# Summing an expert layer back into PSUM and keeping a PSUM bank as scratch for the ordering

## The chip, the cores and the metric

The kernel runs on one core of a Trainium2 chip. The metric is the device time of one execution in microseconds (us). The core's engines work side by side, each through its own list of instructions in order: TensorE (PE in the rows) does matmuls into PSUM, VectorE (DVE) and ScalarE (ACT) read and write SBUF and PSUM, GpSimd (POOL) works on SBUF, SyncE (SP) issues DMAs. An instruction waits for semaphores that others raise.

## The reference

Three parts follow one another: attention with a threshold (2 batches, 8 heads, 576 positions, head size 64), a mixture of experts over the 1152 tokens that come out, and a dense layer with a maximum over three products. The middle one is where the change lies:

```python
def _moe_ref(x, w_gate, w1, w2, capacity):      # x: 1152 x 512, 8 experts, hidden size 1024
    logits = x @ w_gate
    expert_idx = np.argmax(logits, axis=1)
    # softmax; gate_w[i] = probability of the chosen expert
    for i in range(N):                          # tokens take the places of their expert in order
        e = expert_idx[i]
        if counts[e] < capacity:
            disp[e, counts[e]] = x[i]; pos[i] = counts[e]; counts[e] += 1; keep[i] = True
    h = np.maximum(np.einsum('ecd,edf->ecf', disp, w1), 0.0)
    y = np.einsum('ecf,efd->ecd', h, w2)
    # out[i] = gate_w[i] * y[expert_idx[i], pos[i]] for the tokens that are kept
```

## The kernel before

**Stages.** Attention runs to about 190 us. Then comes the routing (gate, places of the tokens), then the ordering: the experts are sorted by a key made of their numbers of tokens, the sorted numbers go into `table`, and lists say which tokens each expert gets. The experts run as eight ranks, `rank(r)` with r from 0 to 7, in the order of the sort; rank r computes `WIN[r]` columns (128, 256, 192, 176, 160, 144, 128, 224 tokens). A branch on a flag, for experts with more tokens than their window, stands ahead of rank 7 (L1333, L1334). The dense stage runs from about 395 us to the end.

**Precision.** Every fp32 operand is split into a rounded high part and a rest, the low part. A product is three matmuls: high weights by high and low data, low weights by high data. Where the columns c are below 256, high and low data lie side by side and one matmul (L1178) fills 2c columns of a PSUM bank, another (L1182) adds the third product to the first c. The two halves of the bank have to be added afterwards. With 256 columns (rank 1) three matmuls (L1180 to L1182) go into the same c columns and nothing is left to add.

**A rank.** Layer 1 has eight pieces f of 128 hidden units (`piece1`), each with a PSUM bank of its own from the pool `ps_h` (six banks, tile `ho`), and four steps k of a matmul pair. `evac1` empties it: ScalarE copies the upper half to `t2` (L1191), VectorE adds the lower half into an SBUF tile `hs` (L1193), and then, two pieces later (the list `later`), ScalarE writes the relu as the high part of `hl` (L1198) and VectorE the low part as max(hs, 0) less the high part (L1199). Layer 2 has four pieces d of eight steps; step k of layer 2 needs piece k of `hl`.

**Weights.** Four 1 MB DMAs a rank (issued by SyncE, tile `raw_w`, three buffers) bring them. Each gives two units: ScalarE rounds the high part (`hi_part`, L872), then VectorE or GpSimd in turn subtracts for the low part (`lo_part`, L877), both into `ring_u`. The DMA of rank r's weights is issued with an expert number read from `table`. After the low part of a unit's second half the next DMA is issued.

**The ordering.** `order1` sorts the experts by counting compares on 8 x 8 matrices (`gtm`, `mr`) up to the CAST into `table` (L739); `spread(1)` has five small matmuls (L629) that build the token map; `order2`, `order2b`, `gates(1)` and `order3` are generators whose steps are laid between the pieces of ranks 0 to 3, one a piece. `order3` ends with ten compare rows (L828) that feed ten small matmuls (L824). The routing has one PSUM bank of its own (`ps_r`, tile `tp`). The order of all instructions is fixed by the order of the code.

Of the kernel before, what the change touches and what calls it, by code (L numbers as in the profile page):

```python
# [76 lines left out]
def fused_kernel(ctx, tc, qk, v, tau, wg, w1, w2, cap, m1, m2, m3, mo, out):  # L77
# [518 lines left out]
    def spread(b):  # L596
# [35 lines left out]
        if b == 0:  # L632
            dve.tensor_copy(tmp0, tm)
            owner.pop()
        else:
# [121 lines left out]
    def order2():  # L757
        f0, f1 = carve([(E, NJ, E), (E, NJ)])
        dve.tensor_tensor(out=f0, in0=tmap.unsqueeze(1).to_broadcast([P, E, NJ, E]),
# [5 lines left out]
        dve.tensor_tensor(out=go, in0=gtm, in1=cnt.unsqueeze(1).to_broadcast([P, E, E]), op=ALU.mult)  # L765
        dve.tensor_reduce(out=off.unsqueeze(2), in_=go, axis=AX.X, op=ALU.add)
        yield
        pick(1, off, rp)
        dve.tensor_copy(table[:, 0, E:2 * E], srt[:, 1])
        yield  # L770

    def order2b():
        pick(2, cnt, rp)
        yield

# [3 lines left out]
        om = smt("om", [P, E])  # L779
# [1 line left out]
        dve.tensor_tensor(out=ov[:, 1], in0=wide(2), in1=st_f, op=ALU.subtract)
        dve.tensor_tensor(out=ov[:, 0], in0=wide(1), in1=st_f, op=ALU.add)
# [2 lines left out]
        dve.tensor_scalar(out=ov[:, 1], in0=ov[:, 1], scalar1=0.0, scalar2=None, op0=ALU.max)
        dve.tensor_scalar(out=ov[:, 0], in0=ov[:, 0], scalar1=float(NT), scalar2=None, op0=ALU.min)
        yield
        om1 = smt("om1", [P, 1])
        dve.tensor_reduce(out=om1, in_=om, axis=AX.X, op=ALU.max)
        dve.tensor_copy(ovt, ov)  # L790
        dve.tensor_copy(flag_t, om1)
# [3 lines left out]
    def order3():  # L795
        n = B * 5
        t2, sl, ge, sg, ind, sp_, gl = carve([(n, E), (n,), (n, NJ + 1), (n,), (n, NJ), (n,), (n, 2)])
# [536 lines left out]
    with tc.If(flag > 0):  # L1334
        iw_i = tq.tile([P, OW], I32, name="mk", bufs=1)
        pool.iota(iw_i, pattern=[[1, OW]], base=0, channel_multiplier=0)
        iw = tq.tile([P, OW], F32, name="hs", bufs=4)
# [11 lines left out]
        def over_chunk(r, m):  # L1349
# [121 lines left out]
```

## Time and profile before

| | |
|---|---|
| median of 3 timed runs | 544.28 us (543.66 to 544.32) |
| profiled execution | 547.7 us, of which the span of the trace is 545.9 |
| busy: TensorE, VectorE, ScalarE, GpSimd | 87%, 67%, 50%, 50% of the span |
| TensorE busy 200 to 226, 250 to 275, 330 to 364 us | 19.33 of 26, 22.01 of 25, 27.45 of 34 us |
| TensorE busy 395 us to the end | 145.34 of 151 us |

How to read the rows. A timeline row has the start in us from the beginning of the span, the duration in us, engine, line, operation, output and inputs by the program's names, shape and count, and in brackets the idle time of the engine just before it with what ended it. A row of waits says which engine's instruction on which tile and line waited for which other one. A row of windows has the stretch and its length, busy time with the number of instructions, the granted clock of TensorE as a share of full speed, the share of the DMA engines' time and GB/s. A group of instructions has the line, the shapes and the count, then busy us and the mean duration in ns, then idle time before. The names: `hl` is the split output of layer 1, `ho` a PSUM bank, `hs` the sum in SBUF, `ring_u` split weights, `table` the sorted expert numbers.

### The profile page before, as it was taken

What the parts mean: (1) busy time and instruction counts of PE and PEld (TensorE: products, weight loads), DVE (VectorE), ACT (ScalarE), POOL (GpSimd) and SP (SyncE); (2) the same over time, 40 slices, a digit from 0 to 9 for tenths busy, and PEclk for the clock granted to TensorE, in tenths of its full rate; (3) what the DMA queues carried; (4) which work ended last, traced back from release to release, by engine and by line L of the source; (5) the groups of instructions that cost most, each with busy time, mean ns of one, the idle gap of its engine ahead of it and who ended that gap; (6) DMA issues with size and microseconds to landing.
All of it is one profiled execution on the core that took longest, in us unless ns stands there. A gap on an engine that the chain in (4) does not pass through costs nothing. (4 is left out here: it accounts for less than half of the span.)

```text
span 545.9 us, 10050 instructions
## 1 busy us (share of the span) xinstructions
PE 477.6 (87%) x3752; PEld 411.9 (75%) x3752; DVE 366.6 (67%) x800; ACT 274.4 (50%) x522; POOL 274.6 (50%) x265
## 2 busy tenths in 40 slices
PE   6688885997785986999799999877999999999995
PEld 4355553674464856999799898777899999999884
DVE  5989989888964249898887867729854454359100
ACT  3879998875644133744466686634412112125211
POOL 3768878886550118572456765646513112217422
PEclk9969999898877577799799999889999999999999
DMA  8577937597598305493737867852024222320111
GB/s 290 120 199 167 202 88 205 127 205 161 114 240 182 112 9 193 155 300 127 246 106 230 272 209 238 278 164 78 1 78 140 91 77 85 148 77 1 58 59 58
DMA packets 105707, 80.42 MB, mean 147 GB/s; under 512 B 66528, under 2 KB 93280, under 8 KB 105392
## 3 DMA queue, kind: packets, MB, share of 16 engines
q1 hardware_dynamic: 100256, 65.97, 42.3%
q10 hardware_dynamic: 3728, 8.47, 5.4%
q0 software_dynamic: 1664, 5.24, 2.7%
q8 instruction: 31, 0.51, 0.4%
q14 instruction: 28, 0.23, 0.1%
HBM read 58.74 MB, written 4.72 MB: 116 GB/s over the span
## 5 line engine op out<-in xcount | busy, mean ns | idle before, releaser
L877 POOL TENSOR_TENSOR ring_u<-raw_w,ring_u 128x1024 fp32r<-128x1024 f32 x32 | 84.5, 2641 | 104.7 <-ACT ring_u L872 102.5
L343 POOL TENSOR_TENSOR phl<-p_t,phl 128x512 f16<-128x512 f32 (+1 forms) x138 | 98.5, 740 | 40.1 <-ACT phl L335 39.8
L1178 PE MATMUL ho<-hl,ring_u 128*128 128x256 f32 (+5 forms) x224 | 69.9, 382 | 12.7 <-DVE hl L1199 11.2
L255 PE MATMUL ps<-kq 64*128 64x288 f32 (+1 forms) x320 | 63.8, 527 | 16.4 <-DVE p_t L280 8.6
L872 ACT ACTIVATE ring_u<-raw_w 128x1024 fp32r<-128x1024 f32 x64 | 66.1, 1054 | 9.2 <-DMA raw_w<-in_moe_w_dram 9.2
L275 ACT ACTIVATE e_t<-ps,negm 128x576 f32<-128x576 f32 x72 | 53.3, 740 | 27.2 <-DVE s_sb L264 24.5
L1140 POOL TENSOR_TENSOR ring_u<-bits_a,ring_u 128x1024 fp32r<-128x1024 f32 x12 | 29.2, 2432 | 74.6 <-ACT ring_u L1139 74.6
L1182 PE MATMUL ho<-hl,ring_u 128*128 128x128 f32 (+6 forms) x256 | 64.8, 253 | 0.0
L264 DVE TENSOR_SCALAR_CACHE_REDUCE s_sb<-ps 128x576 f32<-128x576 f32 x72 | 53.6, 745 | 12.3 <-PE ps L255 12.1
L280 DVE SCALAR_TENSOR_TENSOR p_t<-ps,thr,e_t 128x576 f32<-128x576 f32 x72 | 58.5, 812 | 1.2 <-POOL phl L343 0.6
L1178 PEld LDWEIGHTS ho<-hl,ring_u 128*128 128x128 f32 x224 | 45.7, 204 | 17.5 <-DVE hl L1199 15.0
L1178 PE MATMUL ho<-xl,ring_u 128*128 128x384 f32 (+5 forms) x192 | 55.9, 369 | 3.3 <-DVEq L1334 3.3
L1182 PE MATMUL ho<-xl,ring_u 128*128 128x256 f32 (+6 forms) x224 | 56.9, 254 | 0.0
L387 PEld LDWEIGHTS <-pT 128*128 128x128 f16 x1064 | 41.3, 103 | 16.1 <-issue 9.4
L1182 PEld LDWEIGHTS ho<-hl,ring_u 128*128 128x128 f32 x256 | 52.6, 205 | 0.0
L387 PE MATMUL av<-vah,pT 128*128 128x65 f16 (+1 forms) x684 | 45.2, 202 | 8.0 <-DMA pT<-phl 5.4
L335 ACT ACTIVATE phl<-p_t 128x576 f16<-128x576 f32 x69 | 47.3, 685 | 5.1 <-DVE p_t L280 4.9
L255 PEld LDWEIGHTS ps<-kq 64*128 64x128 f32 (+1 forms) x320 | 25.3, 205 | 27.1 <-DVE p_t L280 10.1
L1182 PEld LDWEIGHTS ho<-xl,ring_u 128*128 128x128 f32 x224 | 44.9, 200 | 0.0
L877 DVE TENSOR_TENSOR ring_u<-raw_w,ring_u 128x1024 fp32r<-128x1024 f32 x32 | 41.1, 1292 | 3.6 <-ACT ring_u L872 3.6
L1178 PEld LDWEIGHTS ho<-xl,ring_u 128*128 128x128 f32 x192 | 38.1, 198 | 4.0 <-ACTq L1334 3.5
L1199 DVE SCALAR_TENSOR_TENSOR hl<-hs,hl 128x128 fp32r<-128x128 f32 (+5 forms) x56 | 36.4, 650 | 5.6 <-ACT hl L1198 5.4
(277 smaller groups left out, 1121.6 us busy)
## 6 DMA issues: line engine op xcount, KB each, us to landing
raw_w<-in_moe_w_dram SPq DMA_DIRECT2D x29, 1024.0 KB, 5.5
raw_w<-in_moe_w_dram SPq DMA_DIRECT2D x18, 512.0 KB, 4.3
kq<-in_qk_dram ACTq DMA_DIRECT2D x3, 1728.0 KB, 7.8
raw_w<-in_moe_w_dram ACTq DMA_DIRECT2D x3, 1024.0 KB, 15.0
raw_w<-in_moe_w_out_dram SPq DMA_DIRECT2D x3, 1024.0 KB, 4.8
raw_w<-in_v_dram SPq DMA_DIRECT2D x2, 1024.0 KB, 10.3
kq<-in_qk_dram SPq DMA_DIRECT2D x2, 864.0 KB, 8.3
xd<-xn SPq DMA_DIRECT2D x1, 1024.0 KB, 5.8
```

What stands on the lines that cost most here:

```text
L255: pe.matmul(o, q[r, hh, t * P:min(t * P + P, S)], q[r, hh, S:S + SH], start=True, stop=True)
L264: dve.tensor_scalar(out=wide(s), in0=s_ps[i][:, :, 0:288], scalar1=-0.125, scalar2=None, op0=ALU.mult, op1=ALU.min, accum_out=m)
L275: act.activation(wide(e), s_ps[i][:, :, 0:288], AF.Exp, bias=negm[i], scale=0.125)
L280: dve.scalar_tensor_tensor(out=wide(p), in0=s_ps.pop(i)[:, :, 0:288], scalar=thr.pop(i), in1=wide(e_t.pop(i)), op0=ALU.is_ge, op1=ALU.mult)
L335: act.activation(phl[i][:, i % 2, 0:S], p_t[i], AF.Copy)
L343: pool.tensor_tensor(out=t[:, lo:hi], in0=p[:, src], in1=t[:, src], op=ALU.subtract)
L387: pe.matmul(o[0:m], pf[:, c * P + off:c * P + off + m], r, start=(n == 0), stop=(n == len(seq) - 1), skip_group_check=True)
L872: act.activation(u[:, 0], w, AF.Copy)
L877: lo_eng(i).tensor_tensor(out=u[:, 1], in0=w, in1=u[:, 0].bitcast(F32), op=ALU.subtract)
L1178: pe.matmul(o[:, 0:2 * c], whi(k), x(k), start=(k == 0), stop=False, skip_group_check=True)
L1182: pe.matmul(o[:, 0:c], wlo(k), x(k)[:, 0:c], start=False, stop=(k == last), skip_group_check=True)
L1199: dve.scalar_tensor_tensor(out=h[:, c:2 * c], in0=src, scalar=0.0, in1=h[:, 0:c].bitcast(F32), op0=ALU.max, op1=ALU.subtract)
```

## The change

The sum of layer 1 goes back into the PSUM bank (`o[:, 0:c]`), and relu and low part read it from there; the SBUF tile `hs` is gone. The bank is held until the low part is written. Seven banks rotate in place of six. The routing's bank `tp` is kept as scratch after the routing: count, token map, a copy of the constant row `iota_p`, the sorted values, offsets, overflow values, keys and gate sums are views of it (`bank`), so that the small operations of the ordering have one input in PSUM; operands change places where needed. ScalarE gets one copy (the constant row), VectorE two (`key` and `ov`, which are needed in SBUF as well).

```diff
     def gate_tail():
         assert not owner
         gate_open(1)
+        bank("ind", 0, 2 * 5, NJ)
+        bank("cnt", 10 * E, E)
+        w = bank("tmap", P, NJ, E)
+        for name, sh in (("iota", (P,)), ("srt", (3, E)), ("off", (E,)), ("om", (E,)), ("sl", (10,)), ("om1", (1,)),
+                         ("su", (5,)), ("key", (E,)), ("k1", (E,)), ("ov", (2, E, NCH))):
+            w = bank(name, w, *sh)
+        assert w <= 512
...
     def order1():
         k0 = smt("k0", [P, E])
-        dve.scalar_tensor_tensor(out=k0, in0=cnt, scalar=8.0, in1=iota_e, op0=ALU.mult, op1=ALU.subtract)
-        yield
-        k1 = smt("k1", [P, E])
+        dve.scalar_tensor_tensor(out=k0, in0=bk["cnt"], scalar=8.0, in1=iota_e, op0=ALU.mult, op1=ALU.subtract)
+        act.activation(bk["iota"], iota_p, AF.Copy)
+        yield
+        k1 = bk["k1"]
...
-        dve.tensor_tensor(out=key, in0=key, in1=k1, op=ALU.add)
-        yield
-        dve.tensor_tensor(out=gtm, in0=key.unsqueeze(1).to_broadcast([P, E, E]),
+        keyp, ie = bk["key"], bk["iota"][:, 0:E]
+        dve.tensor_tensor(out=keyp, in0=k1, in1=key, op=ALU.add)
+        dve.tensor_copy(key, keyp)
+        yield
+        dve.tensor_tensor(out=gtm, in0=keyp.unsqueeze(1).to_broadcast([P, E, E]),
                           in1=key.unsqueeze(2).to_broadcast([P, E, E]), op=ALU.is_gt)
...
-        dve.tensor_tensor(out=mr, in0=pos.unsqueeze(1).to_broadcast([P, E, E]),
-                          in1=iota_e.unsqueeze(2).to_broadcast([P, E, E]), op=ALU.is_equal)
+        dve.tensor_tensor(out=mr, in0=ie.unsqueeze(2).to_broadcast([P, E, E]),
+                          in1=pos.unsqueeze(1).to_broadcast([P, E, E]), op=ALU.is_equal)
...
-        dve.tensor_reduce(out=srt[:, 0].unsqueeze(2), in_=m_, axis=AX.X, op=ALU.add)
-        yield
-        dve.tensor_copy(table[:, 0, 0:E], srt[:, 0])
+        dve.tensor_reduce(out=bk["srt"][:, 0].unsqueeze(2), in_=m_, axis=AX.X, op=ALU.add)
+        yield
+        dve.tensor_copy(table[:, 0, 0:E], bk["srt"][:, 0])
...
-            dve.tensor_scalar(out=am2[:, t % 3], in0=iota_p, scalar1=sp_[:, t:t + 1], scalar2=None, op0=ALU.is_equal)
+            dve.tensor_scalar(out=am2[:, t % 3], in0=bk["iota"], scalar1=sp_[:, t:t + 1], scalar2=None, op0=ALU.is_equal)
...
-    ps_h = ctx.enter_context(tc.tile_pool(name="ps_h", bufs=6, space=PSUM))
+    ps_h = ctx.enter_context(tc.tile_pool(name="ps_h", bufs=7, space=PSUM))
...
             act.activation(t2[:, 0:c], o[:, c:2 * c], AF.Copy)
-            hs_ = tq.tile([P, 256], F32, name="hs", bufs=4)
-            dve.tensor_tensor(out=hs_[:, 0:c], in0=o[:, 0:c], in1=t2[:, 0:c], op=ALU.add)
-            src = hs_[:, 0:c]
-        else:
-            src = o[:, 0:c]
+            dve.tensor_tensor(out=o[:, 0:c], in0=o[:, 0:c], in1=t2[:, 0:c], op=ALU.add)
+        src = o[:, 0:c]
+
         def rest():
             act.activation(h[:, 0:c], src, AF.Relu)
```

The order of instructions changes in two places. The first is VectorE at the end of `order1` and the start of rank 0 (`ring_u` is the low part of a weights unit, `table` the sorted expert numbers, `tp` the routing's bank); before, from the compare `gtm` on:

```order
L725 TENSOR_TENSOR gtm<-key 128x64
L729 TENSOR_REDUCE pos<-gtm 128x8
L731 TENSOR_TENSOR mr<-pos,iota_e 128x64
L735 TENSOR_TENSOR m_3225<-mr,iota_e 128x64
L737 TENSOR_REDUCE srt<-m_3225 128x8
L739 CAST table<-srt 128x8
L877 TENSOR_TENSOR ring_u<-raw_w,ring_u 128x1024
L1193 TENSOR_TENSOR hs<-ho,t_3289 128x128
L877 TENSOR_TENSOR ring_u<-raw_w,ring_u 128x1024
L1193 TENSOR_TENSOR hs<-ho,t_3309 128x128
```

The same stretch of VectorE now:

```order
L748 TENSOR_TENSOR gtm<-tp,key 128x64
L752 TENSOR_REDUCE pos<-gtm 128x8
L754 TENSOR_TENSOR mr<-tp,pos 128x64
L758 TENSOR_TENSOR m_3223<-tp,mr 128x64
L1216 TENSOR_TENSOR ho<-ho,t_3287 128x128
L760 TENSOR_REDUCE tp<-m_3223 128x8
L901 TENSOR_TENSOR ring_u<-raw_w,ring_u 128x1024
L762 CAST table<-tp 128x8
L901 TENSOR_TENSOR ring_u<-raw_w,ring_u 128x1024
L1216 TENSOR_TENSOR ho<-ho,t_3306 128x128
```

The add of piece 0 and one subtraction of weights stand ahead of the CAST now; the subtraction is that of another unit than the one that followed the CAST before.

The second place is TensorE in rank 0, layer 1 (`x_` is the data, `tp<-bm,am` the five matmuls of the token map); before, in piece 0 behind its first pair:

```order
L629 LDWEIGHTS am
L629 MATMUL tp<-bm,am 128x80
L629 LDWEIGHTS am
L629 MATMUL tp<-bm,am 128x80
L1178 MATMUL ho<-x_95,ring_u 128x256
L629 LDWEIGHTS am
L629 MATMUL tp<-bm,am 128x80
L1182 MATMUL ho<-x_95,ring_u 128x128
```

Now, in piece 2, within its third pair (the first two of the five are shown):

```order
L1202 MATMUL ho<-x_92,ring_u 128x256
L1206 MATMUL ho<-x_92,ring_u 128x128
L1202 MATMUL ho<-x_93,ring_u 128x256
L647 LDWEIGHTS am
L647 MATMUL tp<-bm,am 128x80
L647 LDWEIGHTS am
L647 MATMUL tp<-bm,am 128x80
```

The five matmuls have moved back by two pieces, and the first of them waits for the CAST of `table`, which reads the same bank. Elsewhere each engine's instructions stand in the order they had, with `ho` or `tp` in place of an SBUF name.

## Rows read from the trace of the kernel before

**Rows 1.** Windows of TensorE: stretch, length, busy (count), granted clock, DMA share, GB/s.
```profile
395.00:546.00 151.00, 145.34 (x784) 1.00 0.23 79
```

**Rows 2.** TensorE's waits, 200 to 400 us: total us, times, longest.
```profile
PE ho L1178 <- DVE hl L1199: 11.2, 8, 2.7
PE ho L824 <- DVE bits_a L828: 3.4, 3, 2.5
PE ho L1178 <- DVEq L1334: 3.3, 1, 3.3
...
PE ho L1181 <- DVE hl L1199: 1.3, 2, 0.8
```

**Rows 3.** Timeline, VectorE, rank 7: start, duration, operation, idle time before.
```profile
380.06 0.38 DVE L1193 TENSOR_TENSOR hs<-ho,t 128x224 f32<-128x224 f32 x1
380.36 1.20 DVE L1125 TENSOR_SCALAR bits_a<-raw_w 128x1024 int32<-128x1024 int32 x1
381.48 1.20 DVE L1199 SCALAR_TENSOR_TENSOR hl<-hs,hl 128x224 fp32r<-128x224 f32 x1
```

**Rows 4.** Timeline, GpSimd, the same moment.
```profile
379.84 2.58 POOL L1249 TENSOR_TENSOR raw_w<-yT,raw_w 128x384 fp32r<-128x384 f32 x2
```

**Rows 5.** VectorE's groups by shape: busy us, mean ns, idle time before.
```profile
L877 DVE TENSOR_TENSOR ring_u<-raw_w,ring_u 128x1024 fp32r<-128x1024 f32 x32 | 41.1, 1292 | 3.6 <-ACT ring_u L872 3.6
...
L1199 DVE SCALAR_TENSOR_TENSOR hl<-ho,hl 128x256 fp32r<-128x256 f32 x8 | 3.3, 408 | 0.8 <-ACT hl L1198 0.8
...
L1199 DVE SCALAR_TENSOR_TENSOR hl<-hs,hl 128x192 fp32r<-128x192 f32 x8 | 2.8, 348 | 0.2 <-ACT hl L1198 0.2
...
L1193 DVE TENSOR_TENSOR hs<-ho,t 128x192 f32<-128x192 f32 x8 | 2.8, 348 | 2.2 <-ACT t L1191 2.2
```

**Rows 6.** Timeline, TensorE, rank 0: last piece of layer 1, start of layer 2.
```profile
211.57 0.33 PE L1178 MATMUL ho<-x,ring_u 128*128 128x256 f32 x1
...
214.05 0.39 PE L1178 MATMUL ho<-hl,ring_u 128*128 128x256 f32 x1 [1.41 <-DVE hs L1193]
...
215.39 0.58 PE L1178 MATMUL ho<-hl,ring_u 128*128 128x256 f32 x1 [0.89 <-DVE hl L1199]
...
218.73 0.58 PE L1178 MATMUL ho<-hl,ring_u 128*128 128x256 f32 x1 [2.66 <-DVE hl L1199]
```

**Rows 7.** Timeline, VectorE, ordering and rank 0.
```profile
204.37 2.03 DVE L731 TENSOR_TENSOR mr<-pos,iota_e 128x64 f32<-128x64 f32 x1
...
206.94 1.61 DVE L739 CAST table<-srt 128x8 int32<-128x8 f32 x1
...
213.51 0.28 DVE L1199 SCALAR_TENSOR_TENSOR hl<-hs,hl 128x128 fp32r<-128x128 f32 x1
...
216.32 2.36 DVE L1199 SCALAR_TENSOR_TENSOR hl<-hs,hl 128x128 fp32r<-128x128 f32 x1 [0.79 <-ACT hl L1198]
```

**Rows 8.** Timeline, ScalarE, rank 0.
```profile
215.03 1.06 ACT L872 ACTIVATE ring_u<-raw_w 128x1024 fp32r<-128x1024 f32 x1 [4.75 <-DMA raw_w<-in_moe_w_dram]
```

**Rows 9.** Timeline, TensorE, ranks 2, 4, 5, 6 and 7: its longest waits.
```profile
266.00 0.39 PE L824 MATMUL ho<-bits_a 128*128 128x30 f32 x1 [2.45 <-DVE bits_a L828]
...
311.60 0.41 PE L1178 MATMUL ho<-hl,ring_u 128*128 128x320 f32 x1 [0.80 <-DVE hl L1199]
...
330.55 0.41 PE L1178 MATMUL ho<-hl,ring_u 128*128 128x288 f32 x1 [1.09 <-DVE hl L1199]
...
349.74 0.39 PE L1178 MATMUL ho<-hl,ring_u 128*128 128x256 f32 x1 [2.65 <-DVE hl L1199]
...
380.19 0.47 PE L1178 MATMUL ho<-hl,ring_u 128*128 128x448 f32 x1 [2.30 <-DVE hl L1199]
```

**Rows 10.** Windows of TensorE: the stretches at half the granted clock.
```profile
214.60:224.80 10.20, 6.76 (x31) 0.50 0.73 253
265.80:272.60 6.80, 6.61 (x25) 0.50 0.61 203
351.10:354.50 3.40, 3.40 (x18) 0.50 0.87 283
```

More of the change, by code (lines that the diff above doesn't have):

```diff
@@ L89, in fused_kernel @@
     gk = const.tile([P, B, 5], F32, name="gk")
-    off = const.tile([P, E], F32, name="off")
     cnt = const.tile([P, E], F32, name="cnt")
-    srt = const.tile([P, 3, E], F32, name="srt")
     gtm = const.tile([P, E, E], F32, name="gtm")
@@ L486, in gate_part, with bank @@
         yield
+    bk = {}
+    def bank(name, at_, *sh):
+        w = 1
+        for x in sh:
+            w *= x
+        v_ = rt_tp[1][:, at_:at_ + w]
+        if len(sh) == 2:
+            v_ = v_.rearrange("p (a b) -> p a b", a=sh[0])
+        elif len(sh) == 3:
+            v_ = v_.rearrange("p (a b c) -> p a b c", a=sh[0], b=sh[1])
+        bk[name] = v_
+        return at_ + w
     def gate_tail():
@@ L635, in spread @@
         else:
-            dve.tensor_tensor(out=tmap, in0=tm, in1=tmp0, op=ALU.add)
+            dve.tensor_tensor(out=tm, in0=tm, in1=tmp0, op=ALU.add)
         yield
     def gates(b):
-        su = smt("su", [P, 5])
+        su = bk["su"] if b else smt("su", [P, 5])
         dve.tensor_reduce(out=su.unsqueeze(2), in_=ex[b], axis=AX.X, op=ALU.add)
@@ L645, in gates @@
         gt = smt("gt", [P, 5])
+        if b:
+            gt = su
         dve.reciprocal(out=gt, in_=su)
@@ L686, in apart @@
         done.append(i)
-    ov = const.tile([P, 2, E, NCH], F32, name="ov")
+    ov = const.tile([P, E, NCH], F32, name="ov")
     ovt = const.tile([P, 2, E, NCH], I32, name="ovt")
@@ L694, in pick @@
         m_ = pool_.tile([P, E, E], F32, name=f"m_{n}", bufs=1)
-        dve.tensor_tensor(out=m_, in0=mr, in1=col.unsqueeze(1).to_broadcast([P, E, E]), op=ALU.mult)
-        dve.tensor_reduce(out=srt[:, n].unsqueeze(2), in_=m_, axis=AX.X, op=ALU.add)
+        dve.tensor_tensor(out=m_, in0=col.unsqueeze(1).to_broadcast([P, E, E]), in1=mr, op=ALU.mult)
+        dve.tensor_reduce(out=bk["srt"][:, n].unsqueeze(2), in_=m_, axis=AX.X, op=ALU.add)
     def gather(x, idx, src=xd):
@@ L758, in order2 @@
         f0, f1 = carve([(E, NJ, E), (E, NJ)])
-        dve.tensor_tensor(out=f0, in0=tmap.unsqueeze(1).to_broadcast([P, E, NJ, E]),
+        dve.tensor_tensor(out=f0, in0=bk["tmap"].unsqueeze(1).to_broadcast([P, E, NJ, E]),
                           in1=mr.unsqueeze(2).to_broadcast([P, E, NJ, E]), op=ALU.mult)
@@ L764, in order2 @@
         go = rp.tile([P, E, E], F32, name="go")
[L765 to L766 removed]
+        dve.tensor_tensor(out=go, in0=bk["cnt"].unsqueeze(1).to_broadcast([P, E, E]), in1=gtm, op=ALU.mult)
+        dve.tensor_reduce(out=bk["off"].unsqueeze(2), in_=go, axis=AX.X, op=ALU.add)
         yield
[L768 to L769 removed]
+        pick(1, bk["off"], rp)
+        dve.tensor_copy(table[:, 0, E:2 * E], bk["srt"][:, 1])
         yield
     def order2b():
[L773 removed]
+        pick(2, bk["cnt"], rp)
         yield
+        srt, om, op_ = bk["srt"], bk["om"], bk["ov"]
         def wide(n):
             return srt[:, n].unsqueeze(2).to_broadcast([P, E, NCH])
[L779 removed]
         dve.tensor_tensor(out=om, in0=srt[:, 2], in1=wn, op=ALU.subtract)
[L781 to L782 removed]
+        dve.tensor_tensor(out=op_[:, 1], in0=wide(2), in1=st_f, op=ALU.subtract)
+        dve.tensor_tensor(out=op_[:, 0], in0=wide(1), in1=st_f, op=ALU.add)
         yield
         dve.tensor_scalar(out=om, in0=om, scalar1=0.0, scalar2=None, op0=ALU.max)
[L785 to L786 removed]
+        dve.tensor_scalar(out=op_[:, 1], in0=op_[:, 1], scalar1=0.0, scalar2=None, op0=ALU.max)
+        dve.tensor_scalar(out=op_[:, 0], in0=op_[:, 0], scalar1=float(NT), scalar2=None, op0=ALU.min)
         yield
[L788 to L791, printed above, removed]
+        dve.tensor_reduce(out=bk["om1"], in_=om, axis=AX.X, op=ALU.max)
+        dve.tensor_copy(flag_t, bk["om1"])
+        dve.tensor_copy(ovt, op_)
+        dve.tensor_copy(ov, op_[:, 1])
         dve.tensor_copy(omt, om)
@@ L800, in order3 @@
         gkf = gk.rearrange("p b t -> p (b t)")
-        dve.tensor_tensor(out=t2, in0=oh.rearrange("p b t e -> p (b t) e"),
-                          in1=off.unsqueeze(1).to_broadcast([P, n, E]), op=ALU.mult)
+        dve.tensor_tensor(out=t2, in0=bk["off"].unsqueeze(1).to_broadcast([P, n, E]),
+                          in1=oh.rearrange("p b t e -> p (b t) e"), op=ALU.mult)
         dve.tensor_copy(glr[:, :, 0], gkf)
@@ L1336, in fused_kernel @@
         pool.iota(iw_i, pattern=[[1, OW]], base=0, channel_multiplier=0)
-        iw = tq.tile([P, OW], F32, name="hs", bufs=4)
+        iw = tq.tile([P, OW], F32, name="iw", bufs=1)
         dve.tensor_copy(iw, iw_i)
@@ L1352, in over_chunk @@
             mk = tq.tile([P, OW], I32, name="mk", bufs=1)
-            dve.tensor_scalar(out=mk, in0=iw, scalar1=ov[:, 1, r, m:m + 1], scalar2=None, op0=ALU.is_lt)
+            dve.tensor_scalar(out=mk, in0=iw, scalar1=ov[:, r, m:m + 1], scalar2=None, op0=ALU.is_lt)
             for j in range(OW // P):
```

6 lines of the change are left out of this document (3 added, 3 removed).

## Prediction

> **What bounds the kernel now.** I read the busy time of TensorE by stretch first. From 395 us to the end of the span it is busy 145.34 of 151 us at full clock [rows 1]: the dense stage is bound by its own work, and the change leaves it alone. The attention stage up to 200 us is not touched either. So I looked only at 200 to 395 us, routing and experts, and asked TensorE's list of waits there what ended them [rows 2]: 11.2 us in 8 waits end with L1199 (the low part of the first layer's output), 3.4 us with L828 (the comparison rows of the last ordering step), 1.3 us with L1199 again in rank 1; one more of 1.41 us with the add L1193 [rows 6]. All these are VectorE instructions; together 17.3 us. The other large row, 3.3 us at the branch L1334, has nothing to do with them.
>
> Why is VectorE late there? The timeline of rank 7 shows it in four rows. While GpSimd runs its subtraction from 379.84 us on [rows 4], VectorE's add from PSUM takes 0.38 us and its shift of one SBUF tile 1.20 us, but the L1199 at 381.48 us, whose two inputs both lie in SBUF, takes 1.20 us [rows 3] and ends within 0.3 us of GpSimd's. By shape: L1199 takes 348 ns on average at 192 columns, where GpSimd rarely meets it, but one of 128 columns took 2.36 us while GpSimd was at a subtraction, and another 0.28 [rows 7]; at 256 columns, where it reads PSUM already (rank 1), its eight take 408 ns on average [rows 5], not one of them long. So what reads two SBUF tiles stands still until GpSimd's instruction ends, and what reads one of its tiles from PSUM does not.
>
> **The change part by part.** *The add and L1199 through PSUM.* 56 adds now write PSUM, 56 relu and 56 L1199 read it; no instruction is added. Price of one: the add L1193 (PSUM and SBUF in) and L1199 (SBUF twice) both take 348 ns at 192 columns [rows 5], so I count the operand's place at nothing. VectorE writes no PSUM anywhere in the trace; I bound it by nothing on one side and on the other by the difference between 408 ns (256 columns) and 348 ns (192), 60 ns for each of 112 instructions, 6.7 us of VectorE's time, of which most lies under TensorE's matmuls. I take nothing.
>
> [...]
>
> *What goes in the waits, rank by rank.* L828's three waits, 3.4 us, in rank 2: the constant row is read from PSUM now, as are the products ahead of it. All of it goes, since TensorE's matmul came in time whenever L828 was not held up. L1181's 1.3 us in rank 1 (held up: small ordering operations right ahead of L1199): all of it. Ranks 4, 5 and 6: 0.80, 1.09 and 2.65 us [rows 9], each behind one held L1199, 4.5 us; in rank 6 the next pieces follow at VectorE's own pace, so I take 4.3. Rank 7 has 3.1 us (2.30 and two waits of 0.4; 11.2 less the others [rows 2, 6, 9]). There the two conversions of dense weights, 1.2 us each, stay in front of L1199, and the L1199 ahead of 380.19 us also waited for ScalarE: I take 2.0.
>
> Rank 0 is apart. Its waits are 1.41, 0.89 and 2.66 us [rows 6], 5.0 in all. The last ends with the L1199 of 216.32 us, held 2.36 us [rows 7]. But that one could not have begun before ScalarE's relu, and ScalarE stood at 215.03 us, having waited 4.75 us for the weights' DMA [rows 8]. This DMA is issued by SyncE after the CAST of the sorted expert numbers, which was held from 206.94 to 208.55 us, behind the 128x64 compare at 204.37 us that was held 2.03 us [rows 7]. Both read PSUM now: 1.8 and 1.5 us less. Against it the new order puts a weights subtraction ahead of the CAST (1.29 us by L877's mean [rows 5], and its input comes only at 206.3 us from ScalarE): CAST at about 207.65 us instead of 208.55. The weights land 0.9 us earlier, conversion 1.06 us and relu 0.3 us behind, L1199 at about 215.5 to 215.8 us, TensorE goes on at 215.85 instead of 218.73: 2.9 us. Bounds: 2.0 if the DMA comes no earlier, 3.8 if the CAST comes at 206.7.
>
> Sum of the waits: 3.4 + 1.3 + 4.3 + 2.0 + 2.9 = 13.9 us.
>
> *The moved matmuls and the longer hold of banks.* The five matmuls of the token map now stand in piece 2 of rank 0 and wait for the CAST, since they write the bank that is scratch: TensorE gets there at about 207.0 us and waits until 207.65. Behind it stand pieces 2 to 7, 5.0 us at high clock; they end at about 213.1 us, and TensorE would wait until 215.85 anyway. So it costs nothing as long as rank 0's end is set by the DMA; without that cover 0.6 us. ScalarE's new copy of the constant row and VectorE's two extra copies (0.2 to 0.4 us each) fall in VectorE's idle time ahead of 200 us and behind the ordering: nothing. A bank of layer 1 is held until L1199 and not until the add, two pieces longer, with one bank more. In rank 0 piece 7 needs L1199 of piece 0, at about 211.5 us against TensorE's 212.1: just in time. The first pair of layer 2 needs L1199 of piece 1, which the second pair needs in any case: at most one pair, 0.2 to 0.4 us a rank, is late. This goes into the deduction below.
>
> [...]
>
> *The clock.* [...] In rank 2 (265.8 to 272.6 us) TensorE was busy 6.61 of 6.80 us at 0.50; at full clock the same work takes half, 3.4 us less. In rank 6 (351.1 to 354.5 us): 1.7 us less. The stretch of rank 0 (10 us) stays, I think, since a wait of over 2 us stays ahead of it; that behind the branch stays too. So 5.1 us come back if the waits ahead of them go.
>
> *A deduction.* VectorE's own subtraction of weights (L877, two SBUF inputs, 32 times) stays exposed to GpSimd's, and the operation that was held before often stood right next to one. Some of the blocked time moves onto L877, and a later L1199 stands behind it. With the bank's pairs I take 2.0 us off, 0.3 us a rank (bounds: 0 and 7).
>
> Total: 13.9 + 5.1 - 2.0 = 17.0 us. Against the profiled execution, 547.7 us (span 545.9 and 1.8 us around it), this is 530.7. The median of the timed runs is 544.28, 3.4 lower than the profiled one; 544.3 - 17.0 = 527.3 us is my forecast.
>
> **Rivals.**
> (1) The waits go but the clock does not come back, because shorter waits at the same places are enough to drop it. For it: the three stretches follow waits of 2.45 us or more, but no run shows how much less is enough. Against it: ranks 4 and 5 with waits of 0.80 and 1.09 us and rank 7 with one of 2.30 [rows 9] had no such stretch behind them. Gain 13.9 - 2.0 = 11.9: 532.4 us.
> (2) The block moves to L877. VectorE's L877 meets GpSimd's and each L1199 queued behind it is as late as before: ranks 4 to 7 keep their 6.3 us and rank 6 its low clock. Left are 3.4 + 1.3 + 2.9 - 2.0 and, at best, the 3.4 of rank 2's clock: 5.6 to 9.0, middle 7: 537 us. For it: 32 L877 on either engine. Against: those 32 took 1292 ns on average, hardly longer than the 1.20 us of the one-input shift [rows 3, 5], so either engine mostly found the gaps of the other.
> (3) The change does not do what it says: an instruction with one PSUM input is held too. Against it stand the clean instructions [rows 3, 5]. Then nothing but order moves: 544 us.
> (4) Slower: holding the banks. If L1199 is still held (as in 3), piece 7 waits for L1199 of piece 0: in rank 0 that came at 213.8 us [rows 7] while TensorE began piece 7 at 211.57 [rows 6]. Price up to 2.2 us in rank 0 and up to a piece (1.0 us) in each of the other six ranks below 256 columns, 8 at most, half of it likely: 548.5 us. It decides once L1199 of piece 0 ends later than piece 6's matmuls; in the trace this is so in rank 0 alone.
>
> **How the numbers follow.** Forecast (waits and clock) 0.53; (1) 0.22; (2) 0.16; (3) 0.04; (4) 0.05. The forecast's own range is 524 to 531 us: the bounds of rank 0 (-0.9, +0.9), of the deduction (-2, +5 with part of it in rival 2), and, below it, a clock that comes back in rank 0 too (up to 5 us). Taken out to rivals 1 and 2 until two in ten are left: 521.5 to 537.0. A measurement of this kernel tells 0.2%, 1.1 us, from no change. Faster by more: the forecast, (1) and (2), and a little of (3), 0.92; within: 0.04; slower: 0.04.
>
> **What would show it right or wrong.** In the profile after: no L1199 (at its new line) and no comparison row above 0.5 us; the row of TensorE's waits for L1199 down from 11.2 to about 3 us, in ranks 0 and 7 only, and that for the comparison rows gone. The CAST of the expert numbers near 207.65 us and ScalarE's wait for the weights behind it ending near 214.1. Granted clock 1.0 in rank 2 and at the end of rank 6. VectorE's L877 longer than its 1.29 us on average by some tenths; if by 1 us or more, rival 2. The forecast is wrong if long L1199 remain (rival 3), or if TensorE waits for L1199 at the start of a piece 7 (rival 4), or if a wait for weights takes their place on ScalarE, which now gets to them earlier.

## The result and the profile after

The changed kernel took 525.82 us in the median of four runs (522.17 to 530.23), the one before 544.3: 18.5 us less. The ratio, 0.9638 with a 95% interval of 0.9592 to 0.9685, leaves out the run of 530.23 us, which was in a slower state. The forecast was 527.3. The profiled execution has a span of 524.9 us against 545.9.

I cut both spans at the first expert matmul of each rank and at the first matmul of the dense stage (read from TensorE's timeline):

| us | ahead of the experts | 0 | 1 | 2 | 3 | 4 | 5 | 6, branch | 7 | dense, end |
|---|---|---|---|---|---|---|---|---|---|---|
| before | 203.19 | 26.09 | 26.37 | 26.60 | 19.92 | 19.05 | 18.01 | 24.60 | 26.44 | 155.63 |
| after | 197.29 | 25.03 | 24.34 | 20.07 | 18.70 | 17.97 | 16.08 | 26.33 | 23.42 | 155.67 |
| difference | -5.90 | -1.06 | -2.03 | -6.53 | -1.22 | -1.08 | -1.93 | +1.73 | -3.02 | +0.04 |

The experts' stage (ranks 0 to 7) took 187.08 us and takes 171.94: 15.1 less. The 5.9 us ahead of it are looked at below. The dense stage is the same to 0.04 us.

TensorE's waits in the stage, after (what waited, for what: us in total, times, longest), answering [rows 2]:

```profile
PE ho L1202 <- DVEq L1356: 7.6, 1, 7.6
PE tp L647 <- DVE table L762: 4.8, 1, 4.8
PE ho L1191 <- DMA xr<-xd,xidx: 1.7, 2, 1.2
...
PE ho L1202 <- DVE hl L1221: 0.3, 1, 0.3
```

The 11.2 us for the low part (now L1221) are 0.3, the row for the comparison rows (now L852) is gone. Two rows are new or larger: the token-map matmuls L647 wait 4.8 us in rank 0, and the branch takes 7.6 us in place of 3.3.

VectorE's groups by shape, after (busy us, mean ns, idle time before), answering [rows 5]:

```profile
L901 DVE TENSOR_TENSOR ring_u<-raw_w,ring_u 128x1024 fp32r<-128x1024 f32 x32 | 48.8, 1525 | 3.5 <-ACT ring_u L896 2.9 <-issue 0.6
...
L1221 DVE SCALAR_TENSOR_TENSOR hl<-ho,hl 128x128 fp32r<-128x128 f32 x16 | 4.6, 286 | 3.1 <-ACT hl L1220 3.0
L852 DVE TENSOR_SCALAR bits_a<-tp,bits_a 128x128 fp32r<-128x128 f32 x10 | 3.4, 341 | 0.0
...
L1221 DVE SCALAR_TENSOR_TENSOR hl<-ho,hl 128x256 fp32r<-128x256 f32 x8 | 3.3, 414 | 1.0 <-ACT hl L1220 1.0
...
L1216 DVE TENSOR_TENSOR ho<-ho,t 128x192 f32<-128x192 f32 x8 | 2.8, 354 | 0.8 <-ACT t L1215 0.8
L1221 DVE SCALAR_TENSOR_TENSOR hl<-ho,hl 128x192 fp32r<-128x192 f32 x8 | 2.8, 347 | 0.3
```

Every group of the low part is at its undisturbed time: 286 ns at 128 columns, 347 at 192, where the SBUF form had 348. The add that writes PSUM takes 354 ns against 348. So for these two the operand's place costs nothing that can be told.

Counted one by one: before, 12 of the 56 low parts with both inputs in SBUF overlapped a subtraction by GpSimd, and all 12 took 1.01 to 3.00 us; the other 44 took 276 to 393 ns. Now 35 of these 56 overlap one, and none takes more than 392 ns.

The comparison rows are a case of their own: they have one tensor (the constant row) and one scalar a partition. Before and now (count, duration min/median/max in ns, first and last start):

```profile
L828 DVE TENSOR_SCALAR bits_a<-iota_p,bits_a x10: 270/276/2420, 261.7 to 281.6; 128x128 fp32r<-128x128 f32 x10
```

```profile
L852 DVE TENSOR_SCALAR bits_a<-tp,bits_a x10: 336/341/349, 250.2 to 266.1; 128x128 fp32r<-128x128 f32 x10
```

Before, the three that overlapped a subtraction by GpSimd took 2.36 to 2.42 us and the other seven 270 to 279 ns; from PSUM all ten take 336 to 349. With the constant row in PSUM these take about 65 ns more each (341 against 276), 0.7 us for the ten, against some 6 us of blocked time.

VectorE's own subtraction of weights, which still reads two SBUF tiles, went from 1292 to 1525 ns: 32 times 0.23, 7.5 us of blocked time that moved there.

Granted clock by stretch, after (length, TensorE busy, clock, DMA share, GB/s): rank 2, rank 6, the branch, rank 7, and the half-clock stretch behind the branch, answering [rows 10]:

```profile
246.70:266.70 20.00, 20.00 (x146) 1.00 0.68 229
319.50:338.20 18.70, 17.17 (x146) 1.00 0.81 269
338.20:345.80 7.60, 0.03 (x1) 0.74 0.63 205
345.80:369.20 23.40, 23.39 (x128) 0.87 0.14 47
...
341.80:352.00 10.20, 6.19 (x21) 0.50 0.14 44
```

Rank 2, with 6.8 us at half clock before, is at 1.00 and busy all 20.00 us; rank 6 is at 1.00 too. Behind the branch the half clock now lasts 10.2 us; before it lasted 3.4, from 364.7 to 368.1 us.

What went the other way is in rank 0. VectorE, after (start, duration, operation), answering [rows 7]:

```profile
197.16 5.35 DVE L636 TENSOR_SCALAR am<-iota_h,rm 128x128 f16<-128x128 f16 x5
200.22 2.29 DVE L748 TENSOR_TENSOR gtm<-tp,key 128x64 f32<-128x64 f32 x1
...
203.54 2.30 DVE L901 TENSOR_TENSOR ring_u<-raw_w,ring_u 128x1024 fp32r<-128x1024 f32 x1
205.76 0.15 DVE L762 CAST table<-tp 128x8 int32<-128x8 f32 x1
```

GpSimd at the same time, and TensorE's wait:

```profile
197.81 2.44 POOL L901 TENSOR_TENSOR ring_u<-raw_w,ring_u 128x1024 fp32r<-128x1024 f32 x1 [8.78 <-ACT ring_u L896]
200.18 2.27 POOL L1304 MEMSET yT<- 128x1280 f32 x2
202.41 2.34 POOL L901 TENSOR_TENSOR ring_u<-raw_w,ring_u 128x1024 fp32r<-128x1024 f32 x1
```

```profile
205.97 0.49 PE L647 MATMUL tp<-bm,am 128*128 128x80 f16 x5 [4.78 <-DVE table L762]
```

The five rows `am` of the token map (`iota_h` and one scalar a partition, fp16, in SBUF) took 5.35 us. In the profile before the same five took 0.90 us and ended at 203.94, though GpSimd had begun its subtraction at 203.70; here GpSimd began at 197.81 us while they were under way, and they ended at 202.51, with the memset behind it (200.18 to 202.45). `gtm` stands behind them in the queue, then comes the subtraction of weights that was moved ahead of the CAST, held 2.30 us, and the CAST ends at 205.91 us, 8.6 us after the first expert matmul; before it ended 5.4 us after it. TensorE waits 4.78 us at the moved matmuls. All of rank 0's half clock now falls into layer 1:

```profile
198.40:212.10 13.70, 8.93 (x47) 0.50 0.32 102
```

### The profile page after: what moved, and what is told of

Same layout as the page of the kernel before. It is cut to its first block, busy times and chain, and to the rows that moved or that the text cites. A ratio compares the mean times of both kernels' runs of the same rounds, so it can differ in the third digit from the quotient of the medians.

```text
span 524.9 us, 10086 instructions
## 1 busy us (share of the span) xinstructions
PE 463.1 (88%) x3752; PEld 402.8 (77%) x3752; DVE 340.4 (65%) x802; ACT 273.7 (52%) x523; POOL 278.6 (53%) x265
## 5 line engine op out<-in xcount | busy, mean ns | idle before, releaser
L901 POOL TENSOR_TENSOR ring_u<-raw_w,ring_u 128x1024 fp32r<-128x1024 f32 x32 | 83.2, 2602 | 79.8 <-ACT ring_u L896 77.6
L1206 PE MATMUL ho<-hl,ring_u 128*128 128x128 f32 (+6 forms) x256 | 62.5, 244 | 0.0
L1202 PE MATMUL ho<-hl,ring_u 128*128 128x256 f32 (+5 forms) x224 | 61.8, 354 | 0.3 <-DVE hl L1221 0.3
L261 DVE TENSOR_SCALAR_CACHE_REDUCE s_sb<-ps 128x576 f32<-128x576 f32 x72 | 53.7, 746 | 10.8 <-PE ps L252 10.6
L901 DVE TENSOR_TENSOR ring_u<-raw_w,ring_u 128x1024 fp32r<-128x1024 f32 x32 | 48.8, 1525 | 3.5 <-ACT ring_u L896 2.9
L384 PEld LDWEIGHTS <-pT 128*128 128x128 f16 x1064 | 40.2, 102 | 13.7 <-issue 9.7
L384 PE MATMUL av<-vah,pT 128*128 128x65 f16 (+1 forms) x684 | 44.1, 200 | 5.7 <-ACT av_s L416 2.9
L1206 PEld LDWEIGHTS ho<-hl,ring_u 128*128 128x128 f32 x256 | 49.0, 191 | 0.0
L1202 PEld LDWEIGHTS ho<-hl,ring_u 128*128 128x128 f32 x224 | 42.2, 188 | 1.5 <-PE ho L1206 0.5
L384 PE MATMUL av<-val,pT 128*128 128x65 f16 x380 | 34.9, 199 | 0.0
```

Of the source, the lines that this page charges most:

```text
L261: dve.tensor_scalar(out=wide(s), in0=s_ps[i][:, :, 0:288], scalar1=-0.125, scalar2=None, op0=ALU.mult, op1=ALU.min, accum_out=m)
L384: pe.matmul(o[0:m], pf[:, c * P + off:c * P + off + m], r, start=(n == 0), stop=(n == len(seq) - 1), skip_group_check=True)
L901: lo_eng(i).tensor_tensor(out=u[:, 1], in0=w, in1=u[:, 0].bitcast(F32), op=ALU.subtract)
L1202: pe.matmul(o[:, 0:2 * c], whi(k), x(k), start=(k == 0), stop=False, skip_group_check=True)
L1206: pe.matmul(o[:, 0:c], wlo(k), x(k)[:, 0:c], start=False, stop=(k == last), skip_group_check=True)
```

## The experiments

All stage times are from one profiled execution each, cut as above; the totals are from timed runs. Before: 187.1 us (stage). Totals of one kernel varied by up to 16 us between runs, so the stage is the surer measure.

**The changed kernel again.** No edit, two more profiles.

> The changed kernel once more, beside the others on one chip. The first profile had the token-map rows (am, five fp16 operations on VectorE) at 5.35 us instead of 0.90 and TensorE waiting 4.78 us behind them, and 7.58 us at the branch instead of 3.31. Theory: am loses a race of a few tenths of a us against GpSimd's weights subtraction, every time or often; expect am at 5 us and the branch between 3.5 and 7.6 us, 522 to 528 us. Rival: both are accidents of one execution; then am near 1 us and the branch near 3.5, and about 518.

> The changed kernel, timed beside the one with the token-map rows from PSUM. Theory: experts' stage 170 to 172 us, token-map rows held again (about 5 us), 523 to 527 us in all. Rival: rows not held in this execution, stage 167 us.

524.17 us median (520.66 to 531.59) and 526.88 (517.22 to 531.98). Stage 169.6 and 172.4 us; `am` held in both (7.2 and 7.3 us for the ten instructions of both batches, of which the undisturbed first five make 1.9), TensorE's wait behind it 4.4 and 6.0, the branch 5.5 and 7.4. So the changed kernel's stage is 170 to 172 us, and the lost race is the rule.

**One part alone: the layer's sum in PSUM.** The kernel before with the new `evac1` and seven banks.

```diff
+            dve.tensor_tensor(out=o[:, 0:c], in0=o[:, 0:c], in1=t2[:, 0:c], op=ALU.add)
+        src = o[:, 0:c]
```

> Only the sum of layer 1 in PSUM and 7 banks; the ordering's small operations stay in SBUF. Theory (two SBUF inputs are held by GpSimd): ranks 3 to 7 gain as in the full change, about 9 us of waits and clock, rank 0's third wait (2.7 us) goes, and the waits for L828 in rank 2 (3.4 us and 3 us of clock) stay: 533 to 536 us. Rival (the gain comes from the ordering's operations alone): 541 to 544 us.

539.87 us (536.21 to 544.29), ratio 0.9895 [0.9758, 1.0032]; stage 181.0, 6.1 less than before. TensorE's waits:

```profile
PE ho L1178 <- DVEq L1332: 5.8, 1, 5.8
PE tp L629 <- DVE gtm L725: 4.2, 1, 4.2
PE ho L824 <- DVE bits_a L828: 3.5, 3, 2.4
PE ho L1167 <- DMA xr<-xd,xidx: 3.0, 2, 2.2
PE ho L1181 <- DVE xl L1171: 2.1, 1, 2.1
...
PE ho L1178 <- DVE hl L1197: 0.7, 2, 0.5
```

The waits for the low part went from 11.2 to 0.7 us; those for the comparison rows stayed (3.5), and rank 2 with them at 25.99 us. The second row is `am`, held here as well; the profile names `gtm`, which stands behind it. Rank 1, which has no sum to add, became 1.5 us slower: a new wait of 2.1 us for the low part of its own input, which stood behind a CAST into `table` that took 2.18 us under a subtraction by GpSimd. The total missed the 533 to 536 us I expected, and since the interval of its ratio includes 1, it shows no gain by itself; what tells the theory from the rival is the profile.

**The other part alone: the routing's bank as scratch.** The changed kernel with the old `evac1`.

```diff
-            dve.tensor_tensor(out=o[:, 0:c], in0=o[:, 0:c], in1=t2[:, 0:c], op=ALU.add)
-        src = o[:, 0:c]
+            hs_ = tq.tile([P, 256], F32, name="hs", bufs=4)
+            dve.tensor_tensor(out=hs_[:, 0:c], in0=o[:, 0:c], in1=t2[:, 0:c], op=ALU.add)
+            src = hs_[:, 0:c]
+        else:
+            src = o[:, 0:c]
```

> Only the routing's bank as scratch (and 7 banks); the layer's sum stays in SBUF. Theory: ranks 1 and 2 gain 2 and 6.5 us as in the full change, rank 0 none, ranks 3 to 7 keep their waits for the low part: 535 to 538 us. Rival (what was freed is only passed on to the next operation with two SBUF inputs, which are the low parts here): 541 to 546 us.

539.78 us (532.95 to 547.87), ratio 0.9919 [0.9875, 0.9964]; stage 182.4, 4.7 less. VectorE's groups:

```profile
L1223 DVE SCALAR_TENSOR_TENSOR hl<-hs,hl 128x192 fp32r<-128x192 f32 x8 | 6.0, 746 | 0.3 <-ACT hl L1222 0.3
...
L852 DVE TENSOR_SCALAR bits_a<-tp,bits_a 128x128 fp32r<-128x128 f32 x10 | 3.4, 340 | 0.0
```

The comparison rows are free (340 ns), but the low part at 192 columns, which took 348 ns in the kernel before [rows 5], takes 746: in rank 2 it inherited the blocked time. TensorE waited 8.0 us for the low part, and 1.5 us still for the comparison rows. The total lies between the theory's 538 and the rival's 541 us; the rival was half right. The parts alone give 6.1 and 4.7 us, together 10.8; both at once give 14.7 to 17.5. Without the wait at the branch, which is another matter (3.3 us before, 5.8 and 3.5 in the parts, 5.5 to 7.6 with both), it is 8.6 and 4.8 against 18.8 to 19.7. What one part freed was caught by the next instruction that GpSimd held, and only with both parts is none left near TensorE's path but the subtraction of weights and, as below, the rows `am`.

**The contender taken away, in both kernels.** GpSimd writes the same tiles, but reads no SBUF; its memset takes 0.96 us in the median, where the subtraction took 2.34 to 3.34.

```diff
-        lo_eng(i).tensor_tensor(out=u[:, 1], in0=w, in1=u[:, 0].bitcast(F32), op=ALU.subtract)
+        if lo_eng(i) is pool and i > 3:
+            pool.memset(u[:, 1].bitcast(F32), 0.0)
+        else:
+            lo_eng(i).tensor_tensor(out=u[:, 1], in0=w, in1=u[:, 0].bitcast(F32), op=ALU.subtract)
```

> The kernel before, with nothing in PSUM that was not there; GpSimd's weights subtractions from the fifth unit on are replaced by a memset of the same tile (the low parts that GpSimd makes are zero, so part of the product is left out): GpSimd still writes as much but reads no SBUF. Theory (GpSimd's reads hold VectorE's second SBUF input): no low part L1199 above 0.5 us, TensorE's waits for L1199 and the comparison rows fall from 17 us to under 4, experts' stage (first expert matmul to dense stage) 187 us before, now 168 to 173. Rival (what counted was the change's order, banks or the PSUM operand itself): L1199 still long, stage at 182 or more.

> The changed kernel with GpSimd's weights subtractions from the fifth unit on replaced by a memset, as in the same experiment on the kernel before (low parts that GpSimd makes are zero; part of the product is left out). Theory (the change is worth something only because GpSimd's reads hold VectorE): without those reads the change gains nothing, experts' stage 160 to 164 us against 162.4 for the kernel before with the memset. Rival (banks, order or PSUM operands gain or cost something by themselves): more than 3 us away from 162.4 on either side.

Stage 162.4 us for the kernel before, less than the 168 to 173 I expected, and 160.9 for the changed one: without GpSimd's subtractions the change is worth 1.5 us, with them 15 to 17. In the kernel before with the memset (VectorE by shape, and the comparison rows one by one):

```profile
L1202 DVE SCALAR_TENSOR_TENSOR hl<-hs,hl 128x224 fp32r<-128x224 f32 x8 | 5.8, 729 | 1.2 <-ACT hl L1201 1.2
...
L1202 DVE SCALAR_TENSOR_TENSOR hl<-hs,hl 128x128 fp32r<-128x128 f32 x16 | 4.6, 286 | 2.0 <-ACT hl L1201 2.0
...
L828 DVE TENSOR_SCALAR bits_a<-iota_p,bits_a 128x128 fp32r<-128x128 f32 x10 | 3.5, 351 | 0.0
...
L1202 DVE SCALAR_TENSOR_TENSOR hl<-hs,hl 128x192 fp32r<-128x192 f32 x8 | 2.8, 351 | 0.4 <-ACT hl L1201 0.4
```

```profile
L828 DVE TENSOR_SCALAR bits_a<-iota_p,bits_a x10: 274/278/1015, 252.8 to 268.7; 128x128 fp32r<-128x128 f32 x10
```

Nothing is in PSUM that was not there before, and the low part takes 286 ns all the same. The one group that is still long, 729 ns at 224 columns, is rank 7, where GpSimd's other subtractions of two SBUF tiles (L1140 and L1249 of the kernel before) were left in; my "no low part above 0.5 us" failed there. Rank 7 alone differs by 1.8 us between the two kernels (25.0 against 23.2); the other ranks together differ by 0.3 the other way. TensorE's waits for the low part are 2.3 us here, and none for the comparison rows is left.

Since the memset is shorter too, the stages alone do not tell whether it is the reads or the time that GpSimd is at work. The single instructions do: 14 low parts overlapped a memset here, and none took more than 348 ns, while the three that overlapped a subtraction, in rank 7, took 1.20 to 1.55 us. For the low part this settles the mechanism. The comparison rows are different: one that began just behind the start of a memset (265.38 to 266.35 us) took 1015 ns, the other nine at most 280. What holds them is not the reads alone.

The changed kernel gains by the memset as well, 171.9 to 160.9 us: 5.0 of the 11 us are in rank 0, 5.3 in rank 6 with the branch. So what GpSimd's subtractions still cost there is not small.

**Banks.** Seven in the kernel before, six in the changed one.

> The kernel before with seven banks rotating in place of six, nothing else. Theory: no bank is waited for, since the waits end with VectorE's low part; experts' stage within 2 us of 187 and the waits for L1199 near 11 us. Rival (the seventh bank gives part of the gain): stage at 184 or less.

> The changed kernel with six banks in place of seven, each still held until the low part is written. Theory: in a rank piece 6 now waits for the low part of piece 0 and the first pair of layer 2 for that of piece 2, which the third pair needs in any case: up to 0.5 us a rank, experts' stage 171 to 175 us (changed kernel 170 to 172). Rival (the longer hold is dangerous): over 178 us.

Stages 188.9 us against 187.1, and 171.1 against 169.6 to 172.4: nothing is gained by the seventh bank or lost by the sixth that these profiles can tell. Of the first difference 1.2 us are in rank 0. The first of the two also shows that the held `am` is no work of the change:

```profile
204.52 5.30 DVE L618 TENSOR_SCALAR am<-iota_h,rm 128x128 f16<-128x128 f16 x5
207.53 2.29 DVE L725 TENSOR_TENSOR gtm<-key 128x64 f32<-128x64 f32 x1
```

The profile before had won the race. In ten profiles `am` is in SBUF; in two of them GpSimd had the memset in place of the subtraction, and `am` took 1.4 us. Of the other eight seven had lost the race, two of them with the old routing (this kernel and the layer's sum alone). In all eight the last of the five rows and GpSimd's subtraction begin within 5 ns of each other. So the profile that the prediction was worked out from was the exception.

**The rows `am` from PSUM.**

```diff
-            dve.tensor_scalar(out=am[:, t], in0=iota_h, scalar1=rm[:, t:t + 1], scalar2=None, op0=ALU.is_equal)
+            dve.tensor_scalar(out=am[:, t], in0=bk["iota"] if b else iota_h, scalar1=rm[:, t:t + 1], scalar2=None, op0=ALU.is_equal)
```

> The changed kernel, but the five token-map rows (am) read the copy of the constant row in PSUM, fp32, instead of the fp16 one in SBUF. Theory: they are no longer held (0.3 us each, 1.6 in all instead of 5.35), the CAST of the expert numbers comes some 3.3 us earlier, TensorE's wait of 4.8 us behind it shrinks under 1.5 us, rank 0 ends 3 to 4 us earlier: 521 to 523 us, 3 to 4 below the changed kernel. Rival: rank 0's end is set by the weights' DMA in any case: within 1 us of it.

> The changed kernel with the token-map rows from PSUM once more, timed beside the changed kernel. Theory: experts' stage 168 us, rank 0 about 22.2 us; total 2 to 3 us below the changed kernel, if the attention ahead of it, whose end varied from 193 to 205 us between executions, does not hide that. Rival: no difference in the total.

Stage 168.1 and 164.9 us, rank 0 22.2 and 20.7 against 25.0 to 25.3:

```profile
195.34 1.38 DVE L636 TENSOR_SCALAR am<-tp,rm 128x128 f16<-128x128 f32 x5
...
197.61 1.86 DVE L901 TENSOR_TENSOR ring_u<-raw_w,ring_u 128x1024 fp32r<-128x1024 f32 x1
...
200.23 0.17 DVE L762 CAST table<-tp 128x8 int32<-128x8 f32 x1
```

`am` takes 1.38 us though GpSimd's subtraction ran from 195.99 to 198.39 us; the CAST ends 4.9 us after the first expert matmul, and the wait at the token map is 0.2 us. The stage is 1.5 to 7.0 us below that of the changed kernel's first two profiles. The two kernels below have `am` in PSUM too, with rank 0 at 22.3 and 24.2 us. The totals, 525.73 us (521.02 to 531.08) beside 524.17 and 525.83 (523.55 to 537.24) beside 526.88, do not show the 3 to 4 us I expected: what lies ahead of the experts varied by more. I count it as a gain in the stage and as unsettled in the total.

**The branch.** Two tries at the loads that are under way there, both with `am` from PSUM.

```diff
+        pre.clear()
+        for u in held2:
+            dma2(u)
         cv.append(convert2())
```

> The changed kernel with the token-map rows from PSUM, and with the loads of dense weights that were issued ahead of the branch issued right behind it. Theory: TensorE restarts late behind the branch (5.5 to 7.6 us, before 3.3) because the next instructions are fetched by DMA behind 512 KB loads; without these the wait is 3 to 4 us, experts' stage 164 to 166 us against 168.1 with the rows alone, 519 to 523 us. Rival 1: the wait at the branch has another cause and stays at 5 to 7.6. Rival 2: the loads come too late and the dense stage or rank 7 waits for weights, 2 us or more back.

523.61 us (519.87 to 531.21), stage 168.2, wait at the branch 7.7 us. It did not do what it says: SyncE still issued the four loads ahead of its branch (328.98 to 333.24 us, branch at 333.3), so it tells nothing.

```diff
+        if u < 2:
+            pool.memset(w.bitcast(F32), 0.0)
-        if u < 9:
+        elif u < 9:
```

> The changed kernel with the token-map rows from PSUM, and the first two tiles of dense weights filled by a GpSimd memset instead of their four loads of 512 KB, which were under way at the branch (their part of the dense stage is zero). Theory: the wait of TensorE at the branch, 7.5 us, is the fetch of the code behind it, queued behind those loads; without them 3 to 4.5 us. Rival: the wait does not hang on the loads and stays at 5.5 us or more.

The wait is 3.0 us, the shortest of 14 profiles (3.0 to 8.0). VectorE's branch and its next instruction, in the kernel before, in the changed kernel and then here (count, duration ns, first and last start us):

```profile
L1334 DVEq EVENT_SEMAPHORE  x2: 21/21/21, 363.7 to 363.8; - x2
L1334 DVEq COMPARE_BRANCH  x1: 72/72/72, 360.3 to 360.3; - x1
```

```profile
L1356 DVEq EVENT_SEMAPHORE  x2: 21/21/21, 345.6 to 345.8; - x2
...
L1356 DVEq COMPARE_BRANCH  x1: 72/72/72, 339.1 to 339.1; - x1
```

```profile
L1358 DVEq EVENT_SEMAPHORE  x2: 21/21/21, 344.4 to 344.5; - x2
...
L1358 DVEq COMPARE_BRANCH  x1: 72/72/72, 341.3 to 341.3; - x1
```

From the branch to the next instruction VectorE needs 6.5 us in the changed kernel and 3.1 here; before it was 3.4. The DMA traffic in the 2 us ahead of the branch and in the 2 us behind it, changed kernel, then without the loads:

```profile
337.00:339.00 2.00, 1.00 1.07 376
339.00:341.00 2.00, 1.00 0.89 268
341.00:343.00 2.00, 0.70 1.04 347
343.00:345.60 2.60, 0.50 0.04 11
```

```profile
339.30:341.30 2.00, 0.96 0.03 8
341.30:343.30 2.00, 1.00 0.04 12
```

VectorE goes on 2.6 us after the loads have ended (share 0.04 from 343 us). But the kernel before has the same four loads. What differs is when SyncE issues the last two of them, before and then now:

```profile
360.37 1.37 SPq L1114 DMA_DIRECT2D raw_w<-in_moe_w_dram  x2
```

```profile
338.22 0.92 SPq L1138 DMA_DIRECT2D raw_w<-in_moe_w_dram  x2
```

Before, they come just behind VectorE's branch (360.32 us), now 0.9 us ahead of it (339.13). All 14 profiles divide like this: where the last two loads come behind VectorE's branch (the kernel before with six and with seven banks, and the bank alone) or are not there, VectorE needs 3.1 to 3.5 us to its next instruction; in the ten where they come ahead of it, 4.4 to 6.5. So the way over the branch was longer wherever these two loads had been issued ahead of it. That it is the fetch of code, queued behind them, is my reading. The traces have two DMA queues of the kind "instruction"; from VectorE's branch to its next instruction these moved 7 packets in the changed kernel (339.13 to 345.6 us, 0.07 MB) and 3 in the kernel before (360.32 to 363.7, 0.02 MB). Which engine's code that was, and whether VectorE waited for it, they do not say, and no run separates my reading from another cause that hangs on DMA traffic. The run is one execution, and rank 6 had 2.5 us of another DMA wait in it.

## Why the prediction was right, step by step

- **VectorE held by GpSimd's reads**: right for the low part, shown by the 12 held (1.01 to 3.00 us) and the 35 free instructions (at most 392 ns) and by taking the reads away (at most 348 ns under a memset). As a rule, "what reads two SBUF tiles stands still" is too narrow: the comparison rows (2.36 to 2.42 us), the CASTs into `table` (1.61 and 2.18) and `am` (5.35 for its five) read one tensor from SBUF, and they were held as well.
- **PSUM operands at nothing**: right for the low part and the add, 347 ns against 348 and 354 against 348; not for the comparison rows, 341 against 276. Why these alone took 65 ns more, no run tells.
- **Rank 2, 3.4 us of waits and 3.4 of clock**: 6.53 measured, clock 1.00.
- **Rank 1, 1.3 us**: 2.03. **Ranks 4 to 6, 4.3 and 1.7 of clock**: ranks 3 to 6 without the wait at the branch gave 1.22 + 1.08 + 1.93 + 2.54 = 6.8. **Rank 7, 2.0**: 3.02, though 6.2 us of it ran at half clock behind the branch, before 3.4.
- **Rank 0, 2.9 us**: failed. The step that failed is "CAST at about 207.65 us instead of 208.55": relative to the first expert matmul it ended 3.3 us later, not 0.9 earlier, and ScalarE's wait for the weights ended 14.6 us after that matmul, before 11.8. I had taken `am` (0.90 us) for safe since it was short in the one profile, though it reads SBUF just as GpSimd starts. Rank 0 gained 1.1 us none the less: its three old waits, 4.96 us, are gone for one of 4.78, and TensorE's busy time fell from 21.13 to 20.21 us, with 8.9 us of it at half clock in place of 10.2. "So it costs nothing" for the moved matmuls, 0.6 us without cover, was 4.8 us of wait. Some of that is covered after all: with `am` from PSUM TensorE waits 2.1 us in rank 0 for low parts instead.
- **The clock in rank 0 stays**: right in its length, 13.6 us at half before and 13.7 now, but read wrongly. Rival (1) has all three stretches behind waits of 2.45 us or more; that of rank 0 began at 214.6 us [rows 10], behind a wait of 1.41 [rows 6]. A fourth stretch, 204.3 to 207.7 us, was overlooked.
- **The branch stays at 3.3 us**: failed, 7.6, and 5.5 and 7.4 in the other two profiles. The step is that it "has nothing to do with them": I had read the wait as fixed and made no term of it. What the runs show in its place is that it goes with the loads issued ahead of VectorE's branch; why, stays open.
- **The deduction of 2.0 us for L877**: the blocked time did move there (7.5 us), and alone each part showed it at other instructions; with both parts it met TensorE little.

In the stage the sum of 17.0 us met 15.1, 17.5 and 14.7 in three profiles. For the first: the two failed terms lost 1.8 and 4.3 us; the deduction that was not needed (2.0) and what ranks 1, 3 to 6 and 7 gave above their terms (0.7, 0.8 and 1.0) brought most of it back, less 0.3 in rank 2. So the mechanism was right, and the closeness of the sum is in part luck.

The remaining 5.9 us of the profiled difference lie ahead of the experts and belong to no term of the prediction, so that the total came within 1.5 us of the forecast is in part luck too. The 0.2% that the prediction gives a measurement was too little as well: totals of the kernel before ran from 538.6 to 554.4 us. TensorE does the same matmuls there, ten of them (L580) in 4.82 us in this one profile before and 2.62 after. The start of the experts varied from 193 to 205 us over 14 profiles: 199.4 to 205.1 in the four with the old routing, 193.1 to 202.2 in the ten with the bank. Whether the difference of the means (203.1 and 197.8) is chance or comes from the changed routing stays open.

## What to carry to other kernels

Where VectorE waits for GpSimd, count the instructions near the path that GpSimd holds, here those with two SBUF inputs (the low parts, 1.01 to 3.00 us in place of 276 to 393 ns) and also small ones with one (comparison rows, 2.36 to 2.42 us in place of 270 to 279 ns; CASTs, 1.61 and 2.18 in place of 0.17), and move them together: with the routing's bank alone as scratch the blocked time went to the low part at 192 columns, 746 ns in place of 348. A short duration in one profile of an instruction that begins when the other engine does is luck until a second profile shows it: `am` took 0.90 us in one of eight and was held in seven. The wait at the branch was no constant here, 3.0 to 8.0 us in 14 profiles: look at which DMAs are issued just ahead of it.

## What the runs showed of the hardware

Which VectorE instructions GpSimd held in these runs depended on what it was doing. Under a memset, which only writes, the low part from SBUF took at most 348 ns (the experiment on the kernel before), and a subtraction of two SBUF tiles ran on in the kernel with `am` from PSUM: 1.86 us from 197.61, ended 1.1 us into the memset that began at 198.33. But the fp16 rows `am` (one SBUF tensor) ended only with the memset, a comparison row took 1015 ns under one, and the CAST at 206.94 us in the kernel before [rows 7] ended at 208.55, GpSimd's memset there at 208.53. One SBUF tensor alone is not what decides: the int32 shift of [rows 3] took 1.20 us while GpSimd was at a subtraction of 2.58. What sets `am`, the comparison row and the CAST apart from that shift, no trace here shows.
